# Interleaved sequence tails with whole-tile stores, and one PSUM copy moved forward, in a convolution and channel-mix kernel

## The chip, the cores and the metric

The kernel runs on one core of a Trainium2 chip. The metric is the device time of one execution in microseconds (us). The profiler records a single execution; its span runs from the first to the last instruction of the program. In the tables and views, PE is TensorE (PEld its weight loads), DVE is VectorE, ACT is ScalarE, POOL is GpSimd and SP is SyncE; a letter q behind an engine means its instruction queue, such as a DMA issue.

## The reference: what is computed

The input x has 8 sequences of 4160 tokens with 192 channels in float32. First comes a causal convolution of width 7 whose weights are a softmax, one row for each of 8 heads of 24 channels; then a channel mix.

```python
w = softmax(weight, axis=-1)                     # 8 heads x 7 taps
y[b, s, h, g] = sum_k w[h, k] * x_pad[b, s + k, h, g]    # 6 zeros ahead of each sequence
y_prev = y shifted by one token
xk = mu_k * y + (1 - mu_k) * y_prev
xr = mu_r * y + (1 - mu_r) * y_prev
k = relu(xk @ w_k)                               # 192 -> 1024
v = (k * k) @ w_v                                # 1024 -> 192
out = sigmoid(xr @ w_r) * v                      # float32
```

## The kernel before

The 8 sequences are handled as 4 pairs. The two sequences of a pair lie in the two halves of the partitions: 64 channels each, three channel groups c. Work on a pair goes in steps of 512 tokens, and each step has 8 slots of k product (two banks of PSUM each). Four slots make a *bundle*, and the program is a list of bundles, written out by hand: `bundle_first`, `bundle_second`, and `bundle_rest(b, ns)` for all the others, from b = 2 on. Each engine runs its instructions in the order in which this code issues them. Tables (`early`, `rq`, `xt`, `mix_a`, `mix_b`, `mix_c`, `vq`, `late`) hold for each bundle what else is to be issued at a given place, and `run(table, b)` issues it.

These parts matter here:

- **The convolution.** `load_x` (L112) brings blocks of x into `xb` by DMAs that POOL issues. `conv_half` (L630) calls `conv_mm` (L295, matmuls on L310) for one half of a unit, and after the second half `conv_out` (L342) has ScalarE copy the result to `y` (L356). A small instruction in ScalarE's queue after the first half (L318) lets the second half go on. From there y goes to `yT`, with channels on the partitions: for most groups by a write to DRAM (`y_write`, L379) and a transposing read (`y_read`, L387), both issued by SP; for group 3 by `tr(g, j)` (L392), that is TensorE transposes into PSUM (L401) and copies out of it (L410). The five blocks of group 3 make two calls: j = 0 with four blocks, copied by ScalarE in two pieces, and j = 1 with one block, copied by VectorE.
- **The mix.** `diff` (L435) subtracts neighbouring tokens, `scale` (L466) multiplies by mu one channel group at a time, `add_y` (L472) adds y. All of it is VectorE's. `y_of` (L421) gives the tokens of a step, shifted by k.
- **The k product.** `k_mm` (L492) on TensorE, `k_relu` (L504) on ScalarE into one of four `k_sb` buffers, and `k_square` (L518) on VectorE into `k2`.
- **The r and v products.** `r` (L549, with the sigmoid on L557), `v_rows` in two halves (L577, with an instruction in ScalarE's queue, L585, between them), and `v_out` (L593), where VectorE multiplies v by r; SP then issues two stores, one for each sequence (L601).
- **The PSUM ring.** `ring` has four buffers, tag "k", each of two banks. k, r, v, the convolution and the transposes all take their place from it, and a new tile waits until the engine that reads the old one is done.
- **The tails.** 4160 is 8 times 512 plus 64, so 64 tokens of each sequence are left. `keep_tail(p)` (L417) has POOL copy them, with the token ahead, to `y_tail` at the end of each pair, and the last step (LAST) computes all four pairs at once: 256 columns, which are pair by pair 64 tokens. `shaped` (L428) gives the mix buffers that form. In the end `v_last` (L606) makes four tiles of 128 rows, k = 0 to 3. Tile k holds two pairs of one sequence place, 64 rows each, so each tile is stored by two DMAs of 64 rows (L620): the lower half by SP, the upper half by ScalarE.

In `bundle_rest` the third bundle (b = 2) differs from the rest: it issues the transposes of group 3 after the first half of v, and the convolution halves later. The issue order before the change was: k product, relu and square of slot 0; the `mix_b` table (for b = 2 two scalings of xk); k product, relu and square of slot 1; r; the first half of v; `tr(3, 0)` and `tr(3, 1)`; the k product and relu of slot 2; a convolution half; the second half of v; two more convolution halves; the `mix_c` table (`add_y` among it); the k product of slot 3; the last convolution half.

Of the kernel before, what the change touches and what calls it, by code (L numbers as in the profile page):

```python
# [8 lines left out]
BF16 = mybir.dt.bfloat16  # L9
# [5 lines left out]
def kernel(  # L15
# [11 lines left out]
    nc = tc.nc  # L27

    B, S, D = x.shape
# [3 lines left out]
    P = 128  # L33
    NF = DF // P
    Q = 64
    NC = D // Q
# [6 lines left out]
    TAIL = S % 128  # L43
    NPAIR = B // 2
# [4 lines left out]
    const = ctx.enter_context(tc.tile_pool(name="const", bufs=1))  # L49
# [10 lines left out]
    for p in range(NPAIR):  # L60
# [5 lines left out]
        for L in sizes:  # L66
            ns = L * NF // STEP
# [3 lines left out]
    T0, LAST = S - TAIL, len(steps) - 1  # L71
# [108 lines left out]
    wr = const.tile([P, NC, D], BF16)  # L180
    wv = const.tile([P, NF, D], BF16)

    y_tail = const.tile([P, NC, NPAIR, TAIL + 2], BF16)

    def load_thirds(w, m, n, cs=slice(0, NC)):
        for st in range(2):
# [99 lines left out]
    ys, yTs, y_drams = {}, {}, {}  # L286
# [8 lines left out]
    def conv_mm(g, c, half):  # L295

        nb = groups[g][2]
        if half == 0:
            if c == 0:
                ys[g] = two.tile([P, GB, 2 * D], BF16, tag="y", name="y")  # L300
            conv_ps[g, c] = ring.tile([P, 2, BANK], FP32, tag="k", name="ps_c")
        unit = conv_units(g)[c]
        last = len(unit[0]) - 1
        banks = conv_ps[g, c][:, :, 0 : nb * 2 * G * (last + 1)].rearrange("p i (n s c) -> p i n s c", n=nb, s=2)
        for k in range(last + 1):
            for i in range(2):
                q = slice(i * Q, (i + 1) * Q)
                bank = (i + half) % 2
                h = unit[bank][k]
                nc.tensor.matmul(  # L310
                    out=banks[:, bank, :, :, k * G : (k + 1) * G],
                    lhsT=toe[q, h, :],
                    rhs=xbs[g][q, :nb, :, h * G : (h + 1) * G],
                    start=half == 0 and k == 0,
                    stop=half == 1 and k == last,
                )
        if half == 0:
            nc.scalar.clobber_nop([nc.scalar.lower_ap(conv_ps[g, c])])  # L318
# [73 lines left out]
    def tr(g, j):  # L392

        p, blk0, nb, _, _ = groups[g]
        ps = ring.tile([P, 2, 2 * BANK], BF16, tag="k", name="ps_t")
        todo = range(4 * j, min(nb, 4 * j + 4))
        view = ps[:, :, 0 : 6 * BLK].rearrange("p b (c i t) -> p b c i t", c=3, i=2)
        for i0 in todo[::2]:
            for c in range(3):
                for i in range(i0, min(nb, i0 + 2)):  # L400
                    nc.tensor.transpose(  # L401
                        out=view[:, (i - 4 * j) // 2, c, i % 2, :],
                        in_=ys[g][:BLK, i, c * P : (c + 1) * P],
                        identity=ident[:BLK, :BLK],
                    )

        for i in todo[::2]:
            n = min(2, nb - i)
            c0 = YC + (blk0 + i) * BLK
            (nc.scalar.copy if g == 3 and j == 0 else nc.vector.tensor_copy)(  # L410
                out=yTs[p][:, :, c0 : c0 + n * BLK].rearrange("p c (n t) -> p c n t", n=n),
                in_=view[:, (i - 4 * j) // 2, :, :n, :],
            )
# [2 lines left out]

    def keep_tail(p):  # L417
        c0 = YC + T0 - 1
        nc.gpsimd.tensor_copy(out=y_tail[:, :, p, 0 : TAIL + 1], in_=yTs[p][:, :, c0 : c0 + TAIL + 1])  # L419

    def y_of(s, cs, k):  # L421

        p, t0, L, _, _ = steps[s]
        if s == LAST:
            return y_tail[:, cs, :, k : k + TAIL]
        return yTs[p][:, cs, YC + t0 - 1 + k : YC + t0 - 1 + k + L]

    def shaped(s, t):  # L428
        return t.rearrange("p c (a t) -> p c a t", t=TAIL) if s == LAST else t

    def diff(s, cs=slice(0, 3)):
        L = steps[s][2]
# [43 lines left out]
    def k_mm(n, cs=range(NC)):  # L476


        s, j = slots[n]
        L = steps[s][2]  # L480
        xk = xks[s]
        if cs[0] == 0 and n not in k_ps:
            k_ps[n] = ring.tile([P, 2, BANK], FP32, tag="k", name="ps_k")
        ps = k_ps[n]
        nf = STEP // L

        for c in cs:
            for f in range(nf):
                fs = slice((j * nf + f) * P, (j * nf + f + 1) * P)
                for i in range(2):  # L490
                    r = slice(i * Q, (i + 1) * Q)
                    nc.tensor.matmul(  # L492
                        out=ps[:, i, f * L : (f + 1) * L],
                        lhsT=wk[r, c, fs],
                        rhs=xk[r, c, :L],
                        start=c == 0 and f == 0,
                        stop=c == NC - 1 and f == nf - 1,
                    )

    def k_relu(n):  # L500
        ps = k_ps.pop(n)
        k_sb = four.tile([P, 2 * STEP], BF16, tag="k_sb", name="k_sb")
        k_sbs[n] = k_sb
        nc.scalar.activation(out=k_sb, in_=ps.rearrange("p a b -> p (a b)"), func=AF.Relu)  # L504

    def k_square(n):
        s, j = slots[n]
        L = steps[s][2]
        k_sb = k_sbs.pop(n)
        if j == 0:  # L510
            k2s[s] = three.tile([P, NF, 2 * STEP], BF16, tag="k2", name="k2")
        nf = STEP // L
        i = k_sb
        o = k2s[s][:, j, :]
        if nf > 1:
            i = k_sb.rearrange("p (b f t) -> p f b t", b=2, f=nf)
            o = k2s[s][:, j * nf : (j + 1) * nf, 0 : 2 * L].rearrange("p f (b t) -> p f b t", b=2)
        nc.vector.tensor_tensor(out=o, in0=i, in1=i, op=ALU.mult)  # L518
# [11 lines left out]
    def v_mm(o, s, t):  # L530
        for f in range(NF):
            nc.tensor.matmul(  # L532
                out=o,
                lhsT=k2s[s][:, f, t * P : (t + 1) * P],
                rhs=wv[:, f, :],
                start=(f == 0),
                stop=(f == NF - 1),
            )
# [48 lines left out]
    def tile_of(s, j, k):  # L587
        return k // 2 * (steps[s][2] // P) + 2 * j + k % 2
# [17 lines left out]
    def v_last(s, j):  # L606

        r_sb = r_sbs.pop((s, j))
        o_sb = three.tile([P, 4, D], FP32, tag="o_sb", name="o_sb")
        for k in range(4):  # L610
            ps = ring.tile([P, 2, BANK], FP32, tag="k", name="ps_v")
            v_mm(ps[:, 0, 0:D], s, tile_of(s, j, k))
            nc.vector.tensor_tensor(  # L613
                out=o_sb[:, k, :],
                in0=ps[:, 0, 0:D],
                in1=r_sb[:, k // 2, k % 2 * D : (k % 2 + 1) * D],
                op=ALU.mult,
            )
            for i in range(2):
                (nc.scalar if i else nc.sync).dma_start(  # L620
                    out=out[2 * (2 * (k % 2) + i) + k // 2, T0:S, :], in_=o_sb[i * TAIL : (i + 1) * TAIL, k, :]
                )


    early, rq, xt, mix_a, mix_b, mix_c, vq, late = ({} for _ in range(8))
# [4 lines left out]
    def conv_half(unit, half):  # L630
        if unit is not None:
            conv_mm(*unit, half)
            if half == 1:
                conv_out(*unit, nc.scalar.copy)

    for g, (p, blk0, nb, fb, on_pe) in enumerate(groups):
# [13 lines left out]
        if g > 4:  # L650

            b = {5: 1, 6: 2, 7: 7}.get(g)
            b = first_bundle[first_step[p]] + (-15, -11, -7, -3)[(g - 6) % 4] if b is None else b
# [38 lines left out]
    def run(table, b):  # L692
        for fn, a in table.get(b, ()):
            fn(*a)
# [110 lines left out]
    def bundle_rest(b, ns):  # L805

        units = xt.get(b, []) + [None, None]
        quad = vq.get(b, [None])[0]
        for n in bundles[b - 1][2:]:
            k_square(n)  # L810
        run(mix_a, b)
        k_mm(ns[0])
        k_relu(ns[0])
        k_square(ns[0])
        run(mix_b, b)
        if b > 2:
            conv_half(units[0], 0)
        k_mm(ns[1])
        if b > 2:
            conv_half(units[0], 1)  # L820
        k_relu(ns[1])
        k_square(ns[1])
        run(rq, b)
        if quad:
            v_rows(*quad, 0)
        if b == 2:
            tr(3, 0)
            tr(3, 1)
        k_mm(ns[2])
        k_relu(ns[2])  # L830
        if b == 2:
            conv_half(units[0], 0)
            v_rows(*quad, 1)
            conv_half(units[0], 1)
            conv_half(units[1], 0)
        else:
            conv_half(units[1], 0)
            if quad:
                v_rows(*quad, 1)
                conv_half(units[1], 1)  # L840
        run(mix_c, b)
        k_mm(ns[3])
        if not quad or b == 2:
            conv_half(units[1], 1)
        k_relu(ns[3])
        if quad:
            v_out(*quad)
        run(late, b)
# [53 lines left out]
```

## Time and profile before

| | us |
|---|---|
| median of 7 runs | 420.02 (419.73 to 421.88) |
| the profiled execution's own time | 419.8 |
| its span in the profile | 418.0 |
| TensorE matmuls busy | 407.5 (97%) |
| VectorE busy | 378.2 (90%) |
| ScalarE busy | 347.8 (83%) |
| GpSimd busy | 49.0 (12%) |

The page gives for each group of instructions its line, engine, operation and tile, the busy time, the mean time of one, and the idle time of that engine just ahead of the group with what ended it. The page also follows the chain of work that ended last back from the last instruction, as shares of the span. The timeline lists instructions in order of time: start, length, engine, line, operation, and in brackets the idle time of the engine ahead of it. Instructions of one engine overlap a little, so a start says more than a start and a length. A DMA has two times: that of its issue in a queue, and that from issue to landing. The rows for the stores at the end and for the y tails are these: the eight stores of L620 are 48 KB each, four from each queue, and land after 1.9 to 2.5 us; the three VectorE operations on `y_tail` take 0.55 to 0.57 us each; the four copies of `keep_tail` take 0.36 to 0.49 us on POOL.

### The profile page before, as it was taken

To read this page: it belongs to the slowest core of one execution; us is meant where nothing else is said; L and a number is where in the kernel's file an instruction comes from. 1 tells how busy PE (TensorE), PEld (TensorE's weight loads), DVE (VectorE), ACT (ScalarE), POOL (GpSimd) and SP (SyncE) were. 2 spreads that over 40 slices of the span, in tenths; PEclk is the share of its full clock that TensorE was granted. 3 is DMA by queue.
4 is the path that set the end of the run, shared out by engine and by line. 5 is a ranking of instruction groups with operands and counts; after the bars stand their busy time and mean duration, and the time that the engine had idled before them with its cause. 6 is when DMAs were issued, how large, how long until landed. Compare 5 with 4: busy or idle time off the path is not lost.

```text
span 418.0 us, 16366 instructions
## 1 busy us (share of the span) xinstructions
PE 407.5 (97%) x7136; PEld 316.1 (76%) x7136; DVE 378.2 (90%) x674; ACT 347.8 (83%) x408; POOL 49.0 (12%) x73
## 2 busy tenths in 40 slices
PE   7989999999999999999999999999999999999995
PEld 3667777777887778778777877777777788777795
DVE  5888799999999999999999999999999999999983
ACT  5989898898898889888888888898898788887771
POOL 6650002102030100202012010201000000000000
PEclk9999999999999999999999999999999999999998
DMA  9998779958599694959769693898945554421124
GB/s 148 193 190 159 186 187 189 232 140 164 132 191 230 155 193 123 146 162 186 180 149 193 182 175 128 146 220 147 179 111 154 144 138 124 118 78 57 60 79 115
DMA packets 134746, 64.59 MB, mean 155 GB/s; under 512 B 84990, under 2 KB 134674, under 8 KB 134674
## 3 DMA queue, kind: packets, MB, share of 16 engines
q1 hardware_dynamic: 95908, 48.28, 44.9%
q0 software_dynamic: 37872, 14.66, 30.8%
q8 instruction: 56, 0.92, 0.9%
q10 hardware_dynamic: 894, 0.61, 0.5%
q14 instruction: 16, 0.13, 0.1%
HBM read 29.89 MB, written 36.99 MB: 160 GB/s over the span
## 4 chain that ended last, share of the span: by engine, by line
PE 90%; ACT 2%; issue 1%; DVE 0%; ACTq 0%
PE ps_v L577 39%; PE ps_k L492 37%; PE ps_r L549 7%; PE ps_c L310 5%; ACT k_sb L504 1%; PE ps_v L532 1%; ACT y L356 0%; DVE o_sb L593 0%; DVE o_sb L613 0%; ACTq L356 0%; ACTq L318 0%; ACTq L585 0%
## 5 line engine op out<-in xcount | busy, mean ns | idle before, releaser
L504 ACT ACTIVATE k_sb<-ps_k 128x1024 bf16<-128x1024 f32 x260 | 260.9, 1039 | 53.2 <-PE ps_k L492 53.1
L492 PE MATMUL ps_k<-xk,wk 64*128 64x512 bf16 (+1 forms) x1632 | 200.2, 367 | 0.7 <-DVE xk L472 0.3
L518 DVE TENSOR_TENSOR k<-k_sb 128x1024 bf16<-128x1024 bf16 x260 | 177.7, 688 | 14.9 <-ACT k_sb L504 7.9
L577 PE MATMUL ps_v<-wv,k 64*128 64x192 bf16 x4032 | 188.8, 243 | 0.6 <-ACT k_sb L504 0.4
L577 PEld LDWEIGHTS <-k 64*128 64x128 bf16 x4032 | 172.4, 94 | 13.7 <-issue 1.4
L492 PEld LDWEIGHTS <-wk 64*128 64x128 bf16 x1632 | 88.0, 94 | 51.1 <-issue 1.2
L593 DVE TENSOR_TENSOR o_sb<-ps_v,r_sb 128x768 f32<-128x768 f32 x64 | 61.3, 957 | 12.4 <-PE ps_v L577 4.9
L557 ACT ACTIVATE r_sb<-ps_r 128x768 bf16<-128x768 f32 x65 | 54.6, 842 | 0.0
L356 ACT CAST y<-ps_c 120x960 bf16<-120x960 f32 (+4 forms) x67 | 50.7, 787 | 3.2 <-PE ps_c L310 3.2
L126 POOL DMA_DIRECT2D xb<-in_x_dram x34 | 30.6, 902 | 194.2 <-PE ps_c L310 93.0
L549 PEld LDWEIGHTS <-xr 64*128 64x128 bf16 x780 | 36.1, 94 | 11.2 <-issue 0.4
L549 PE MATMUL ps_r<-wr,xr 64*128 64x192 bf16 x780 | 44.0, 243 | 0.0
L310 PE MATMUL ps_c<-xb,toe 64*128 64x480 bf16 (+2 forms) x240 | 39.2, 335 | 1.1 <-DVE yT L410 0.8
L466 DVE TENSOR_SCALAR xr<-d,mu 128x512 bf16<-128x512 bf16 (+1 forms) x102 | 35.6, 352 | 0.0
L466 DVE TENSOR_SCALAR xk<-d,mu 128x512 bf16<-128x512 bf16 (+1 forms) x99 | 32.8, 358 | 0.1
L435 DVE TENSOR_TENSOR d<-yT 128x1536 bf16<-128x1536 bf16 (+3 forms) x37 | 31.4, 848 | 0.9 <-ACT yT L340 0.9
L472 DVE TENSOR_TENSOR xr<-xr,yT 128x1536 bf16<-128x1536 bf16 (+1 forms) x33 | 31.0, 940 | 1.1
L472 DVE TENSOR_TENSOR xk<-xk,yT 128x1536 bf16<-128x1536 bf16 (+2 forms) x34 | 30.5, 897 | 0.1
L310 PEld LDWEIGHTS <-toe 64*128 64x128 bf16 x240 | 13.5, 94 | 13.0 <-issue 2.1
L419 POOL COPY y_tail<-yT 128x195 bf16<-128x195 bf16 x4 | 1.8, 456 | 68.5 <-DMA yT<-y_dram 68.5
L108 POOL MEMSET xb<- 32x384 bf16 x3 | 1.2, 408 | 45.0 <-PE ps_k L492 43.7
L330 PEld LDWEIGHTS <-xb 128*32 128x32 bf16 (+3 forms) x264 | 4.3, 102 | 2.7 <-issue 1.7
(52 smaller groups left out, 62.2 us busy)
## 6 DMA issues: line engine op xcount, KB each, us to landing
out_dram<-o_sb SPq DMA_DIRECT2D x128, 192.0 KB, 2.7
y_dram<-y SPq DMA_DIRECT2D x10, 900.0 KB, 6.4
xb<-in_x_dram POOLq DMA_DIRECT2D x14, 480.0 KB, 7.9
xb<-in_x_dram POOLq DMA_DIRECT2D x6, 432.0 KB, 8.2
xb<-in_x_dram POOLq DMA_DIRECT2D x10, 192.0 KB, 5.9
y_dram<-y SPq DMA_DIRECT2D x3, 450.0 KB, 6.1
y_dram<-y SPq DMA_DIRECT2D x1, 810.0 KB, 5.8
wk<-in_moe_w_k_dram POOLq DMA_DIRECT2D x4, 192.0 KB, 6.5
```

The source lines that it names most:

```text
L310: nc.tensor.matmul(out=banks[:, bank, :, :, k * G : (k + 1) * G], lhsT=toe[q, h, :], rhs=xbs[g][q, :nb, :, h * G : (h + 1) * G], start=hal ...
L356: copy(out=bass.AP(tensor=y.tensor, offset=y.offset + d0, ap=[y.ap[0], [d1 - d0, 2], [2 * D, nb], [Q, 2], [1, n]],), in_=bass.AP(tensor=ps ...
L435: nc.vector.tensor_tensor(out=shaped(s, diffs[s][:, cs, :L]), in0=y_of(s, cs, 1), in1=y_of(s, cs, 0), op=ALU.subtract)
L466: nc.vector.tensor_scalar(out=t[:, c, :L], in0=diffs[s][:, c, :L], scalar1=mu[:, i, c : c + 1], scalar2=None, op0=ALU.mult)
L472: nc.vector.tensor_tensor(out=o, in0=o, in1=y_of(s, sl, 0), op=ALU.add)
L492: nc.tensor.matmul(out=ps[:, i, f * L : (f + 1) * L], lhsT=wk[r, c, fs], rhs=xk[r, c, :L], start=c == 0 and f == 0, stop=c == NC - 1 and f ...
L504: nc.scalar.activation(out=k_sb, in_=ps.rearrange("p a b -> p (a b)"), func=AF.Relu)
L518: nc.vector.tensor_tensor(out=o, in0=i, in1=i, op=ALU.mult)
L549: nc.tensor.matmul(out=ps[:, i, k * D : (k + 1) * D], lhsT=xr[q, c, ts], rhs=wr[q, c, :], start=c == 0, stop=c == NC - 1,)
L557: nc.scalar.activation(out=r_sbs[s, j], in_=ps[:, :, 0 : 2 * D], func=AF.Sigmoid)
L577: nc.tensor.matmul(out=v_ps[s, j][:, bank, k * D : (k + 1) * D], lhsT=k2s[s][q, f, t * P : (t + 1) * P], rhs=wv[q, f, :], start=half == 0 ...
L593: nc.vector.tensor_tensor(out=o_sb.rearrange("p (b t) d -> p b (t d)", b=2), in0=v_ps.pop((s, j)), in1=r_sbs.pop((s, j)), op=ALU.mult,)
```

## The change

There are two independent parts.

First, in the third bundle, the square of slot 1 and the `mix_b` table are issued after the two calls of `tr` instead of ahead of r. On VectorE the order from the square of slot 0 on was: two scalings of xk, the square of slot 1, the copy of `tr(3, 1)`, `add_y`. It becomes: the copy, the square of slot 1, the two scalings, `add_y`. The order on the other engines is the same.

Second, the layout of the tails. `y_tail` had the axes channel group, pair, token; it gets channel group, pair of pairs, token, and which of the two. So a column of the last step is (pair of pairs, token, which), and a tile of 128 rows in `v_last` holds the tokens of two pairs in turn. One DMA stores a whole tile, with a DRAM side that steps token by token and inside that between the two sequences. Tiles 0 and 2 are stored by SP, tiles 1 and 3 by ScalarE.

```diff
-    y_tail = const.tile([P, NC, NPAIR, TAIL + 2], BF16)
+    y_tail = const.tile([P, NC, NPAIR // 2, TAIL + 1, 2], BF16)
...
-        nc.gpsimd.tensor_copy(out=y_tail[:, :, p, 0 : TAIL + 1], in_=yTs[p][:, :, c0 : c0 + TAIL + 1])
+        nc.gpsimd.tensor_copy(out=y_tail[:, :, p // 2, :, p % 2], in_=yTs[p][:, :, c0 : c0 + TAIL + 1])
...
-            return y_tail[:, cs, :, k : k + TAIL]
+            return y_tail[:, cs, :, k : k + TAIL, :].rearrange("p c a t b -> p c a (t b)")
...
-        return t.rearrange("p c (a t) -> p c a t", t=TAIL) if s == LAST else t
+        return t.rearrange("p c (a t) -> p c a t", t=2 * TAIL) if s == LAST else t
...
-            for i in range(2):
-                (nc.scalar if i else nc.sync).dma_start(
-                    out=out[2 * (2 * (k % 2) + i) + k // 2, T0:S, :], in_=o_sb[i * TAIL : (i + 1) * TAIL, k, :]
-                )
+            (nc.scalar if k % 2 else nc.sync).dma_start(
+                out=bass.AP(
+                    tensor=out.tensor,
+                    offset=out.offset + ((4 * (k % 2) + k // 2) * S + T0) * D,
+                    ap=[[D, TAIL], [2 * S * D, 2], [1, D]],
+                ),
+                in_=o_sb[:, k, :],
+            )
...
-        run(mix_b, b)
         if b > 2:
+            run(mix_b, b)
             conv_half(units[0], 0)
         k_mm(ns[1])
         if b > 2:
             conv_half(units[0], 1)
         k_relu(ns[1])
-        k_square(ns[1])
+        if b > 2:
+            k_square(ns[1])
         run(rq, b)
         if quad:
             v_rows(*quad, 0)
         if b == 2:
             tr(3, 0)
             tr(3, 1)
+            k_square(ns[1])
+            run(mix_b, b)
         k_mm(ns[2])
```

## The prediction

> **What bounds the kernel now.** I read the page first, then the chain of waits, then the idle time by engine, and then two stretches of the timeline: the third bundle and the end. The page's totals and chain:
>
> ```profile
> span 418.0 us, 16366 instructions
> ...
> PE 407.5 (97%) x7136; PEld 316.1 (76%) x7136; DVE 378.2 (90%) x674; ACT 347.8 (83%) x408; POOL 49.0 (12%) x73
> ...
> PE 90%; ACT 2%; issue 1%; DVE 0%; ACTq 0%
> ```
>
> The reader is to see that TensorE sets the time: 90% of the chain is its work. The chain cut to 60 to 410 us holds TensorE lines alone, and over 28 to 410 us TensorE's idle time, asked by releaser, sums to 0.8 us (0.4, 0.2 and 0.2). So there are two places where time can be had: a stretch in which TensorE stands still, and the stretch after its last matmul, which starts at 413.15 us and ends near 413.4, while the span runs to 418.0. The change touches one of each. The largest single idle stretch of TensorE after 20 us is in the third bundle (TensorE's timeline; start, length, engine, line, in brackets the idle time ahead and what ended it):
>
> ```profile
> 24.72 0.96 PE L401 MATMUL ps_t<-ident,y 120*128 120x120 bf16 x15
> 25.84 0.82 PE L492 MATMUL ps_k<-xk,wk 64*128 64x512 bf16 x6 [0.16 <-ACT r_sb L557]
> 27.50 0.38 PE L310 MATMUL ps_c<-xb,toe 64*128 64x480 bf16 x2 [0.83 <-DVE yT L410]
> 27.70 1.50 PE L577 MATMUL ps_v<-wv,k 64*128 64x192 bf16 x32
> ```
>
> The convolution at 27.50 needs a place in the PSUM ring of four, and takes the one that VectorE's copy of the last transposes (L410) gives back. VectorE's own row of work shows why that copy is late:
>
> ```profile
> 25.27 0.68 DVE L518 TENSOR_TENSOR k<-k_sb 128x1024 bf16<-128x1024 bf16 x1
> 25.87 0.72 DVE L466 TENSOR_SCALAR xk<-d,mu 128x512 bf16<-128x512 bf16 x2
> 26.51 0.68 DVE L518 TENSOR_TENSOR k<-k_sb 128x1024 bf16<-128x1024 bf16 x1
> 27.11 0.33 DVE L410 COPY yT<-ps_t 128x360 bf16<-128x360 bf16 x1
> 27.37 0.95 DVE L472 TENSOR_TENSOR xk<-xk,yT 128x1536 bf16<-128x1536 bf16 x1
> 29.29 0.96 DVE L593 TENSOR_TENSOR o_sb<-ps_v,r_sb 128x768 f32<-128x768 f32 x1 [0.98 <-issue]
> ```
>
> The transposes ended at 24.72 + 0.96 = 25.68; the copy stood behind two scalings and a square until 27.11. VectorE then waits 0.98 us for the v product that the late convolution held up. The end (ScalarE's and SyncE's queues):
>
> ```profile
> 412.05 2.53 ACTq L620 DMA_DIRECT2D out_dram<-o_sb  x4
> ```
> ```profile
> 411.78 0.92 SPq L601 DMA_DIRECT2D out_dram<-o_sb  x2
> 412.79 2.72 SPq L620 DMA_DIRECT2D out_dram<-o_sb  x4
> ```
>
> The last multiplication ends at 413.43 + 0.36 = 413.79. ScalarE issues its last store at 414.02, but SyncE, kept by the v_out pair (L601) until 412.70, then issues four stores of 0.56 to 0.66 us in a row and begins its last one at 414.96. That lands 1.94 us later, at 416.90, and 1.12 us of closing work follow.
>
> **Part 1, the third bundle.** Nothing is added: the order of six VectorE instructions changes, and TensorE, ScalarE and the queues keep theirs. The copy now follows the square at 25.27, so it can start at 25.87, when that one lets go (the transposes ended 0.19 us before). It ends at 25.87 + 0.33 = 26.20, and with the 0.06 us that lay between copy and matmul before (27.11 + 0.33 = 27.44 to 27.50) the place is free at 26.26. TensorE's six k matmuls issue in three steps of about 0.215, until 25.84 + 0.65 = 26.49. So the convolution starts at 26.49 instead of 27.50: **-1.0 us**.
>
> What is late next? (a) The square and the two scalings move 0.26 us later (copy to next start: 27.37 - 27.11). Behind them add_y still starts at 27.37 and ends at 28.32; its reader, the k product of the next bundle, moves from 30.30 to 29.3, so 1 us is left. The square's ScalarE buffer comes round four relus later. (b) VectorE is free at 28.24; the v product's end moves from 29.2 to 28.2, so L593 moves from 29.29 to about 28.3. VectorE's 0.98 us of idle time is just used up: this also caps the gain. (c) ScalarE is busy until 28.03 and then idle for 1.40 us ahead of the y copy at 29.44; that copy can go 1.0 us earlier and leaves 0.4. (d) The x block that this convolution reads: POOL issued its last load at 15.1 and it took 11.0 us, so it landed at about 26.1. The weight load carrying that wait ran at 26.27, 0.10 us behind its neighbour, so it lost nothing; but only some 0.15 us are to spare, where 1.2 us were. If that landing is late by d, the gain is 1.0 - (d - 0.15). Bounds: 1.0 where it isn't late, nothing where it is late by 1.15; the row says it wasn't, so I take 1.0. The other inputs have room: the next x block's loads landed by 30.5, are read at 38.3 and would be read at 37.3.
>
> Is it kept to the end? Between 28 and 60 us TensorE, ScalarE and VectorE wait for one another in turn; each link starts from work that is itself 1.0 us earlier. The one fixed delay inside is the trip of y through DRAM (written at 39.07, read back at 45.12, landed 7.3 us later at 52.4, for a VectorE operation at 53.18); it starts 1.0 us earlier too. From 60 us on the chain is TensorE's alone, and an earlier start is an earlier end.
>
> **Part 2, the tails.** keep_tail on POOL writes every second element: four copies of 0.36 to 0.49 us on an engine that is 12% busy, the last at 361.9 against a reader at 394.8; even ten times that costs nothing. VectorE's three operations on y_tail took 0.57, 0.55 and 0.56 us. The Trainium skill, VectorE: DVE Perf Modes, section "Mode 2×_1P — pack two bf16 into one 32-bit read", asks for step 1 and 4-byte alignment; the old layout reads one operand an odd number of elements off, the new one does not, and by the rule these three would each lose 0.4 us in the old form. The rows differ: 768 elements of yT, with the same odd offset, took 0.55, and 1536 took 0.96, so the slope is 0.41 us for 768, and the odd offset has no slower rate to lose. I take 0. Bounds: one slope, 0.4 us each way for each; all three lie ahead of idle stretches of VectorE (0.76 at 401.15, 1.04 at 406.89) or of an operand needed much later, so also 0 on the path.
>
> The stores: eight become four, k = 0 and 2 on SyncE, 1 and 3 on ScalarE. SyncE: k = 0 at 412.79 as before, k = 2 by 413.6, done by 414.3. ScalarE: the last multiplication ends at 413.79 and 0.23 us later, as before, the last store is issued: 414.02. It is now the last of all. Its landing is not in the trace at this size (96 KB). Nearest rows: the 48 KB stores of this end took 1.94 to 2.47, the 192 KB store at 411.78 took 2.03. I take 2.1, so it lands at 416.1 instead of 416.9: **-0.8 us**; from the ends, -0.4 (2.47) to -0.9 (1.94). For the size alone, the Trainium skill, DMA: Bandwidth & Descriptors, section "Anatomy of one DMA — SWDGE (gpsimd) path", gives 2.0 us and the bytes at 436 GB/s, fitted to another queue; by it a doubled store would land an estimated 0.1 us later and the gain be 0.1 smaller; the 192 KB row shows no such growth.
>
> **Sum.** 1.0 + 0.8 = 1.8 us off the profiled execution's own time of 419.8 (span 418.0 and 1.8 around it): 418.0. The median of the seven runs, 420.02, is 0.2 above that execution, so a median of 418.0 to 418.2; I say 418.1, which is 0.45% less. A measurement of this kernel can tell about 0.3%, 1.26 us, from no change.
>
> **Rivals.**
> 1. *Only one gain counts.* The x block lands late in most executions, or VectorE's copy has to wait for the transposes, and the stall comes back under another name: 419.8 - 0.8 - (0 to 0.4) = 418.6 to 419.2. For: 0.15 us to spare on a load that took 11.0. Against: the weight load did not wait. Or the end falls away and only 1.0 is left: 419.0. Chance 0.30, nearly all within 0.3%.
> 2. *Nothing arrives*: ScalarE or VectorE between 28 and 60 us takes the microsecond back, since VectorE's slack is used up to 0.0, and the new store lands no sooner: 419.4 to 420.0. Against: their idle stretches there (0.2 to 1.2 us) are waits for earlier work that moves too. Chance 0.05.
> 3. *Slower*: the new store, whose DRAM side jumps between two sequences at each row, is not spread over the DMA engines. Its 128 rows of 768 B, at the 0.04 us that such a packet took at the end by the trace's packet records, are 5.1 us on one engine against 0.3 on sixteen: landing 4.8 us later, and 418.0 + 4.8 = 422.8. On n engines it is 5.1/n; the 1.8 us are gone, and it decides, with two engines or fewer. Against: the 48 KB stores of 64 rows kept to 1.94 us, and a first dimension of 64 rows in DRAM and 128 in SBUF is no shorter than theirs. Chance 0.04.
>
> The forecast has 0.61. **Range** 417.6 (both gains at their bounds, 1.0 + 0.9, and 0.3 less for the profiled run's spread) to 419.3 (rival 1 with its ends). Faster by over 0.3%: 0.63; within: 0.33; slower: 0.04.
>
> **What would show it.** Part 1: no idle time ahead of L310 near 26.5, VectorE's copy at 25.9, L593 near 28.3 without a gap, and the last matmul near 412.1 instead of 413.15. If the weight load of L310 waits instead, it is the x block. Part 2: last issue on ScalarE's queue 0.23 us behind the last multiplication, and from that multiplication's end to the span's end 3.4 us instead of 4.2. The prediction is wrong if the last matmul has not moved, or if the store takes over 2.5 us.

## The result, and the profile after

| | before | after |
|---|---|---|
| median, us | 420.05 (419.58 to 422.02, 47 runs) | 418.37 (417.78 to 420.03, 20 runs) |
| span of the profiled execution, us | 418.0 | 416.6 |

The ratio of the two is 0.9959, with a 95% interval of 0.9951 to 0.9967: 0.41% faster, where 418.1 us and 0.45% were forecast. From the page of the changed kernel, the totals and the chain:

```profile
span 416.6 us, 16358 instructions
...
PE 407.4 (98%) x7136; PEld 316.6 (76%) x7136; DVE 379.1 (91%) x674; ACT 347.7 (83%) x408; POOL 49.0 (12%) x73
...
PE 91%; ACT 3%; DVE 3%; issue 1%; POOL 0%; ACTq 0%; POOLq 0%
```

The work is the same to 0.1 us on TensorE; 1.4 us of the span are gone, and they are idle time of TensorE. The third bundle, TensorE's timeline of the changed kernel:

```profile
25.04 0.96 PE L401 MATMUL ps_t<-ident,y 120*128 120x120 bf16 x15
26.16 0.82 PE L492 MATMUL ps_k<-xk,wk 64*128 64x512 bf16 x6 [0.16 <-ACT r_sb L557]
26.81 0.38 PE L310 MATMUL ps_c<-xb,toe 64*128 64x480 bf16 x2
27.01 1.50 PE L577 MATMUL ps_v<-wv,k 64*128 64x192 bf16 x32
```

The bracket behind L310 is gone. From the first transpose to the convolution it was 27.50 - 24.72 = 2.78 us and is 26.81 - 25.04 = 1.76 (with unrounded starts): 1.02 us less. But the transposes themselves stand 0.32 us later than in the profile before, which is why the span shows 1.4 and not 1.8 us; the first experiment asks whose doing that is. VectorE beside it:

```profile
25.59 0.68 DVE L518 TENSOR_TENSOR k<-k_sb 128x1024 bf16<-128x1024 bf16 x1
26.19 0.33 DVE L410 COPY yT<-ps_t 128x360 bf16<-128x360 bf16 x1
26.44 0.68 DVE L518 TENSOR_TENSOR k<-k_sb 128x1024 bf16<-128x1024 bf16 x1
27.04 0.61 DVE L466 TENSOR_SCALAR xk<-d,mu 128x512 bf16<-128x512 bf16 x2
27.68 0.96 DVE L472 TENSOR_TENSOR xk<-xk,yT 128x1536 bf16<-128x1536 bf16 x1
28.60 0.96 DVE L593 TENSOR_TENSOR o_sb<-ps_v,r_sb 128x768 f32<-128x768 f32 x1
```

The copy follows the first square at once, and L593 (v times r) follows `add_y` without its 0.98 us of waiting. The end, ScalarE's queue and then SyncE's:

```profile
411.82 1.87 ACTq L619 DMA_DIRECT2D out_dram<-o_sb  x2
```
```profile
411.09 0.95 SPq L601 DMA_DIRECT2D out_dram<-o_sb  x2
412.14 1.32 SPq L619 DMA_DIRECT2D out_dram<-o_sb  x2
```

Now ScalarE's last store, begun at 413.14, is the last of all, and SyncE is done before it.

To compare executions, four differences are read from each trace: the *bundle stretch*, from the first transpose of the third bundle to the convolution behind it; the *middle*, from there to the start of the last matmul; the *end stretch*, from there to the end of the span; and within that the *closing*, from the last store's landing on. The last matmul's start is near its end, since the closing matmuls follow each other at 0.08 us.

| kernel | first transpose at | bundle stretch | middle | end stretch | last store issued after the last matmul's start | closing |
|---|---|---|---|---|---|---|
| before | 24.72 | 2.78 | 385.65 | 4.87 | 1.81 | 1.12 |
| after | 25.04 | 1.76 | 385.66 | 4.12 | 0.67 | 1.38 |
| after, again | 24.72 | 1.76 | 385.65 | 4.25 | 0.67 | 1.37 |
| after, third time | 24.73 | 2.06 | 385.76 | 4.08 | 0.67 | 1.38 |
| part 1 only | 24.70 | 1.76 | 385.70 | 4.89 | 1.80 | 1.14 |
| part 2 only | 24.49 | 2.74 | 385.69 | 4.06 | 0.67 | 1.37 |
| last store on the last semaphore | 27.02 | 1.77 | 385.70 | 3.67 | 0.67 | 0.95 |
| the same, again | 25.26 | 1.76 | 385.76 | 3.80 | 0.67 | 0.94 |
| copy between | 25.10 | 2.13 | 385.69 | 4.12 | 0.67 | 1.37 |
| old halves, SyncE relieved | 26.88 | 1.76 | 385.71 | 4.64 | 1.52 | 1.19 |

The middle column is the strongest evidence that what the bundle gains is kept: 385.65 to 385.76 us in ten profiles, whatever stands ahead of it.

### The profile page after: what moved, and what is told of

Same layout as the page of the kernel before. It is cut to its first block, busy times and chain, and to the rows that moved or that the text cites. A ratio compares the mean times of both kernels' runs of the same rounds, so it can differ in the third digit from the quotient of the medians.

```text
span 416.6 us, 16358 instructions
## 1 busy us (share of the span) xinstructions
PE 407.4 (98%) x7136; PEld 316.6 (76%) x7136; DVE 379.1 (91%) x674; ACT 347.7 (83%) x408; POOL 49.0 (12%) x73
## 4 chain that ended last, share of the span: by engine, by line
PE 91%; ACT 3%; DVE 3%; issue 1%; POOL 0%; ACTq 0%; POOLq 0%
PE ps_v L577 40%; PE ps_k L492 38%; PE ps_r L549 7%; PE ps_c L310 5%; ACT k_sb L504 2%; PE ps_v L532 1%; DVE k L518 1%; ACT y L356 1%; PE warm L702 1%; DVE d L435 0%; POOL xb L126 0%; ACT yT L340 0%; DVE xk L448 0%; DVE xk L466 0%; DVE xk L472 0%
## 5 line engine op out<-in xcount | busy, mean ns | idle before, releaser
L593 DVE TENSOR_TENSOR o_sb<-ps_v,r_sb 128x768 f32<-128x768 f32 x64 | 61.2, 957 | 11.2 <-PE ps_v L577 4.5
L310 PE MATMUL ps_c<-xb,toe 64*128 64x480 bf16 (+2 forms) x240 | 39.2, 334 | 0.3
L310 PEld LDWEIGHTS <-toe 64*128 64x128 bf16 x240 | 13.5, 94 | 11.8 <-issue 0.9
L330 PEld LDWEIGHTS <-xb 128*32 128x32 bf16 (+3 forms) x264 | 4.8, 109 | 2.5 <-issue 1.5
```

The source lines that it names most:

```text
L310: nc.tensor.matmul(out=banks[:, bank, :, :, k * G : (k + 1) * G], lhsT=toe[q, h, :], rhs=xbs[g][q, :nb, :, h * G : (h + 1) * G], start=hal ...
L593: nc.vector.tensor_tensor(out=o_sb.rearrange("p (b t) d -> p b (t d)", b=2), in0=v_ps.pop((s, j)), in1=r_sbs.pop((s, j)), op=ALU.mult,)
```

## The experiments

### The changed kernel again (after_again)

> The changed kernel once more, beside its parts and on their chip. Its first profile has the 15 transposes of the third bundle at 25.04 us where the kernel before has them at 24.72, although nothing ahead of them differs. Theory A: those 0.32 us are a matter of the single execution (when the first x blocks land); then this profile lies anywhere between 24.7 and 25.1 and the span between 416.3 and 416.7, with 4.1 us from the start of the last matmul to the end. Theory B: the change itself costs them; then 25.04 again, to 0.05. Ratio to before 0.996.

Measured: the transposes at 24.72, span 416.4, ratio 0.9950 (0.9937 to 0.9962). Theory A holds: the 0.32 us belong to one execution. Against the kernel before this profile has 1.6 us less span: 1.01 in the third bundle (the last matmul starts at 412.14 instead of 413.15) and 0.62 in the end stretch.

### Each part alone (part1_only, part2_only)

The two parts of the diff, each taken alone onto the kernel before.

> Only the copy ahead of the square and the two scalings; tails and stores as before. Theory A (the stall at 27.50 was the copy's lateness and its 1.0 us is kept to the end): no idle time ahead of the convolution, 1.77 us from the start of the third bundle's first transpose to the convolution's start (2.78 before), end stretch unchanged at 4.87 us from the last matmul's start; ratio 0.9976, about -1.0 us. Rival (the engines take it back between 28 and 60 us): the stall goes but the ratio stays between 0.999 and 1.0.

> Only the tails; the third bundle as before. Theory A (parts add up): the end stretch is 4.14 us instead of 4.87, so -0.7 us, ratio 0.9983, and the stall of 0.83 us ahead of the convolution is there. Rival (what the first part gives is all there is, the store's gain is lost in its closing): ratio 0.9995 to 1.0.

Part 1 alone: ratio 0.9983 (0.9970 to 0.9997), median 418.95 against 420.14. Its stretches are as expected, 1.76 and 4.89. The ratio is less of a gain than the 0.9976 that was expected, and its interval, which holds that, also reaches into the rival's range (0.999 to 1.0). So the time alone does not settle it; the profile does: the middle is 385.70 us, where the kernel before has 385.65, and nothing was taken back there. TensorE's timeline of part 1 alone, and of part 2 alone:

```profile
24.70 0.96 PE L401 MATMUL ps_t<-ident,y 120*128 120x120 bf16 x15
25.82 0.82 PE L492 MATMUL ps_k<-xk,wk 64*128 64x512 bf16 x6 [0.16 <-ACT r_sb L557]
26.47 0.38 PE L310 MATMUL ps_c<-xb,toe 64*128 64x480 bf16 x2
```
```profile
24.49 0.96 PE L401 MATMUL ps_t<-ident,y 120*128 120x120 bf16 x15
25.61 0.82 PE L492 MATMUL ps_k<-xk,wk 64*128 64x512 bf16 x6 [0.16 <-ACT r_sb L557]
27.23 0.38 PE L310 MATMUL ps_c<-xb,toe 64*128 64x480 bf16 x2 [0.80 <-DVE yT L410]
```

Part 2 alone: ratio 0.9974 (0.9964 to 0.9985), median 419.03; the stall is back and the end stretch is 4.06. The parts add up as far as times known to some 0.1% can show it: 0.17% and 0.26% are 0.43%, against 0.41% measured together. Neither rival is left: the first part's gain is not taken back, by the profile, and the second part's is not lost, by time and profile.

### The copy half way back (copy_between)

```diff
         k_relu(ns[1])
-        if b > 2:
-            k_square(ns[1])
+        k_square(ns[1])
...
             tr(3, 1)
-            k_square(ns[1])
             run(mix_b, b)
```

> The changed kernel, but with the copy behind the square of slot 1 and ahead of the two scalings: half way back. Theory A (the copy's end releases the convolution, one for one past TensorE's own time): the copy starts 0.60 us later, which uses up the 0.23 us between its release and the convolution and then costs 0.37: 2.1 us from the first transpose to the convolution's start (1.76 with the change, 2.78 before), ratio 0.997. Rival (any order with the copy ahead of the scalings does): 1.76 and 0.996.

Measured: bundle stretch 2.13, ratio 0.9973 (0.9958 to 0.9989). TensorE's timeline of this kernel:

```profile
25.10 0.96 PE L401 MATMUL ps_t<-ident,y 120*128 120x120 bf16 x15
26.22 0.82 PE L492 MATMUL ps_k<-xk,wk 64*128 64x512 bf16 x6 [0.16 <-ACT r_sb L557]
27.23 0.38 PE L310 MATMUL ps_c<-xb,toe 64*128 64x480 bf16 x2 [0.19 <-DVE yT L410]
```

Three places of the copy give three stalls: 0.83 behind the scalings and the square, 0.19 behind the square alone, none ahead of both. The bracket counts from the end of the last k matmul, which the profile models; that is 0.17 us later than the next matmul could start, so the loss in starts is 2.13 - 1.76 = 0.37, as worked out beforehand. The ratio's interval holds both 0.997 and the rival's 0.996; it is the stretch that decides.

### The next wait: the x block (xb_late, xb_late_old_order)

The prediction named the x block of the freed convolution as what is late next. A first attempt, wv_twice, issued the load of wv twice in the prologue:

> The changed kernel with the load of wv issued twice in the prologue, ahead of the x block that the freed convolution reads; the second brings the same data again. In the profiles so far that block lands at 25.6 to 26.1 us and wv takes 2.0 us of the queue. Theory A (the block's landing is the next wait, as the rival in the prediction has it): it lands near 27.9, the convolution starts at about 28.1, 3.4 us behind the first transpose, and the ratio goes back to about 0.9995; the weight load of that convolution waits. Theory B (nothing depends on it): 1.76 us and 0.996.

It was a poor experiment: POOL's second load into the same tile had to wait for the first to land (POOL stood still for 6.9 us), and the v product ahead of the transposes then waited itself. From 27.2 us on, behind that wait, TensorE's granted clock was 0.50 for 3.4 us, and the same v product took 2.74 us instead of 1.50. The ratio was 1.0081 (1.0063 to 1.0099), out of what either theory said. TensorE's waits of this kernel, longest first (the columns are the wait in us in total, how many, and the longest):

```profile
PE ps_v L577 <- DMA wv<-in_moe_w_v_dram: 4.1, 1, 4.1
PE ps_c L310 <- DMA xb<-in_x_dram: 0.5, 1, 0.5
```

The second line is the wait that was looked for, but not its price. So the load was repeated into a tile that nobody reads, with the new order and with the old one:

```diff
         load_wv()
+        nc.gpsimd.dma_start(out=spare, in_=moe_w_v.rearrange("(f p) d -> p f d", p=P))
         x_tile(4)
```

> The changed kernel with one more load of w_v, into a tile that nobody reads, just ahead of the x block of the freed convolution: 2.0 us of the queue, so the block should land near 27.7 to 28.3 instead of 25.6 to 26.7, and no product waits for the extra load itself. Theory A (the block's landing is the next wait, one for one): the convolution's weight load waits for it, the convolution starts 0.15 us behind the landing, near 28.1, some 3.3 us behind the first transpose (1.76 with the change), and the ratio goes to about 1.0. Theory B (the block has slack): 1.76 us and 0.996.

> The same extra load in the kernel before. Theory A: the old order waits until 27.5 anyway, so of a landing at 28.1 it loses only some 0.6 us: ratio 1.0015, 3.3 us from the first transpose to the convolution as in the other run (2.78 before). Theory B: 2.78 us and 1.0.

The two timelines, the new order first (the added lines move L310 to L311 and the others alike):

```profile
24.76 0.96 PE L402 MATMUL ps_t<-ident,y 120*128 120x120 bf16 x15
25.88 0.82 PE L493 MATMUL ps_k<-xk,wk 64*128 64x512 bf16 x6 [0.16 <-ACT r_sb L558]
28.23 0.38 PE L311 MATMUL ps_c<-xb,toe 64*128 64x480 bf16 x2 [1.53 <-DMA xb<-in_x_dram]
```
```profile
24.62 0.96 PE L402 MATMUL ps_t<-ident,y 120*128 120x120 bf16 x15
25.74 0.82 PE L493 MATMUL ps_k<-xk,wk 64*128 64x512 bf16 x6 [0.16 <-ACT r_sb L558]
28.49 0.38 PE L311 MATMUL ps_c<-xb,toe 64*128 64x480 bf16 x2 [1.93 <-DMA xb<-in_x_dram]
```

The block landed at 28.10 and at 28.36, and each convolution began 0.13 us behind. Theory A holds: one for one, and with the block this late both orders wait for the same thing and part 1 is worth nothing. The stretches are 3.47 and 3.87 us, where 3.3 was expected for both; they differ by as much as the landings do against the transposes. The ratios agree with it: 1.0004 (0.9990 to 1.0017) with the change and 1.0021 (1.0005 to 1.0038) without, 0.17% apart, which is what the end stretch alone (some 0.75 us) would leave, though the intervals overlap.

This also happens by itself. In the other profiles of the same prologue, those with the table's first transposes below 26 us, the block landed between 25.6 and 26.7. The third profile of the changed kernel had the latest, and there it cost 0.30 us; TensorE's weight loads in that execution:

```profile
25.62 0.56 PEld L492 LDWEIGHTS <-wk 64*128 64x128 bf16 x6
26.76 0.13 PEld L310 LDWEIGHTS <-toe 64*128 64x128 bf16 x2 [0.58 <-issue]
```

The weight load of L310, which had run 0.10 us behind the end of its neighbours in the kernel before, stood until 26.76, 0.1 us behind the landing at 26.66; so the bundle stretch is 2.06 and not 1.76.

### SyncE's queue or the stores' size (halves_relieved)

Part 1 with the old layout and its eight half-tile stores, of which ScalarE takes five:

```diff
-                (nc.scalar if i else nc.sync).dma_start(
+                (nc.scalar if i or k == 0 else nc.sync).dma_start(
```

> Part 1 with the old layout and the old eight half-tile stores, but ScalarE issues both stores of tile 0, so that SyncE, kept by the pair ahead, has three left and not four. Theory A (the end was late by SyncE's queue of issues, not by the stores' size): ScalarE issues five at about 0.65 us each, the last begins 1.45 us behind the last matmul's start instead of 1.80; 4.55 us to the end where part 1 alone has 4.89, so 0.3 us less than that, ratio 0.9975. Rival (it is the number or size of the stores that lands late): 4.9 us still, last landing over 2.3 us.

Measured: ratio 0.9967 (0.9954 to 0.9979), last store 1.52 us behind the last matmul's start, end stretch 4.64 against 4.89 of part 1 alone. The last store landed after 1.9 us, as before. So the old end was late by the issues in line on a queue: one store less in the longer line was worth 0.25 us in the profile, with no change of a store's size or of their number. The ratio alone would not tell it, since its interval overlaps with that of part 1 alone (0.9970 to 0.9997). ScalarE's queue of this kernel and of part 1 alone:

```profile
413.25 3.17 ACTq L620 DMA_DIRECT2D out_dram<-o_sb  x5
```
```profile
411.07 2.53 ACTq L620 DMA_DIRECT2D out_dram<-o_sb  x4
```

Five stores in 3.17 us and four in 2.53: 0.63 each. This shows a step of the prediction to be wrong: with four, ScalarE's last store does not begin 0.23 us behind the last multiplication because a signal takes that long, but because the one ahead of it has just been issued (before the change that one held the queue from 413.36 to 413.93, and the last began at 414.02). With two stores in ScalarE's queue it begins 0.03 us behind (413.11 to 413.14).

### The order of the closing waits (lane_last, lane_again)

A semaphore tells SyncE that a store has landed; the stores take eight semaphores in turn, and at the close SyncE waits for all eight. The run is the changed kernel, with seven 4 KB stores to scratch tensors added late in the kernel, in the sixty-first bundle:

```diff
+        if b == 60:
+            for i in range(7):
+                nc.sync.dma_start(out=pads[i][:, :], in_=ident[:, 0:16])
```

> The changed kernel with seven stores of 4 KB to a scratch tensor late in the kernel, which move the last store from semaphore 0 of the eight that the stores take in turn to semaphore 7. At the close SyncE waits for the eight one after the other, some 0.06 us each; in the changed kernel the last landing (415.20) is that of the first of them, and 1.40 us follow to the end, 1.12 before the change. Theory A (the order of these waits is what the end lost): some 1.0 us from the last landing to the end, so 0.4 us less than the changed kernel, ratio 0.995. Rival (the closing is as long wherever the last store stands): 1.4 us, ratio 0.996, or worse by what the seven stores cost.

Measured: closing 0.95, end stretch 3.67; in the second run 0.94 and 3.80. In the page's terms, SyncE's instructions behind the last landing, in the changed kernel and in this one (second run):

```profile
L904 SPq EVENT_SEMAPHORE  x10: 17/28/28, 415.2 to 416.5; - x10
```
```profile
L909 SPq EVENT_SEMAPHORE  x3: 17/17/28, 415.7 to 416.5; - x3
```

Ten against three, and 7 at 0.06 us are 0.43. Before the change it was six (closing 1.12), and with ScalarE's five stores it was seven (closing 1.19); both lie on the same line. So theory A holds in the profile. In the time it is not settled. The first run had a ratio of 0.9949 (0.9933 to 0.9966) and a median of 417.99 against 418.10 of the changed kernel on the same chip; it was repeated beside the changed kernel:

> The kernel with the last store on the last of the eight semaphores once more, beside the changed kernel on one chip. If the order of the closing waits is worth its 0.4 us in the unprofiled time too: median 0.4 us under the changed kernel's, ratio 0.995 against 0.996. If the spread of the prologue (24.5 to 27.0 us at the first transpose in the profiles so far) hides it, the medians differ by under 0.2 us, and only the end stretch tells (3.7 us against 4.1 to 4.25).

> The changed kernel, for comparison with the kernel beside it: ratio 0.9955, end stretch 4.1 to 4.25 us.

Medians 418.21 against 418.45, ratios 0.9955 (0.9943 to 0.9968) and 0.9962 (0.9948 to 0.9975). Both comparisons point the same way, by 0.11 and 0.24 us where the profiles say 0.43, and the intervals overlap: that this kernel is the faster of the two is likely and not shown.

## Why the prediction was right, point by point

**The bundle, -1.0 us: right in place, mechanism and size.** The stretch fell by 1.01 to 1.02 us in the undisturbed profiles, the copy began when the first square let go, and L593's gap closed. The item-by-item search for what is late next held: `add_y`, ScalarE and VectorE were in time, and the x block, with its 0.15 us to spare, was the next wait; it took 0.30 us back in one profile of the changed kernel out of three. That rival was real, as a part of the spread and not as the rule.

**Kept to the end: right.** The middle is the same in all profiles to 0.1 us.

**The end, -0.8 us: right in sum, by luck: two errors nearly cancel.** From the last matmul's start, the last issue was forecast at 0.87 us (414.02 - 413.15) and came at 0.67, since ScalarE's own line of issues had been taken for a signal's delay. The landing was forecast at 2.1 and took 2.0 to 2.2. The closing was taken to stay at 1.12 us and took 1.37 to 1.38: the last store now stands first in SyncE's list of waits. In sum -0.62 to -0.81 against the kernel before. The rule that was weighed for the landing, the Trainium skill's DMA: Bandwidth & Descriptors, section "Anatomy of one DMA — SWDGE (gpsimd) path", had an estimated 0.1 us for the doubled size. The last 48 KB stores took 1.93 to 1.95 and the last 96 KB ones 2.0 to 2.2, so the doubled size came with 0.1 to 0.3 us. By that estimate a last store would take 2.04 us (1.94 + 0.1), by the 192 KB row 2.03: both lie at the low end, so the runs do not choose between them.

**The tails' layout, 0: right, with one reading wrong.** VectorE's three operations took 0.55, 0.55 and 0.56 us (0.57, 0.55 and 0.56 before). The prediction has all three read an operand an odd number of elements off in the old layout. By the code only `diff` did (its operand with k = 1); the two `add_y` read k = 0, at even places in both layouts. So the alignment that the skill's VectorE: DVE Perf Modes asks for is tried by one operation, and it went from 0.57 to 0.55 us, not by 0.4; POOL's copies with their step of two took 0.41 to 0.43.

**The slower rival did not come**: the stores to two sequences in turn land like the others.

**418.1 against 418.37.** The measured terms add to 1.5 to 1.8 us in the three profiles of the changed kernel, where 1.8 was forecast, and the first medians differ by 1.68. What is left is within what one median differs from the next (418.37, 418.10 and 418.45 for the same kernel).

## What to carry to other kernels

Where one engine bounds the kernel, look for the few stretches in which it stands still, and for who gives back the buffer it waits for; an instruction that frees a shared buffer belongs ahead of work with slack on its engine, and the price can be read off beforehand, down to where the next wait caps it. At the end of a kernel, count the issues in line on each queue behind the last result, not the bytes: here one 96 KB store on a free queue beat two of 48 KB behind others. And before a gain of that kind is booked, look for the input that had slack only because of the stall that is to go.

## What the runs showed of the hardware that was not expected

- At the close SyncE waits for the stores' eight completion semaphores one after another, about 0.06 us each, in a fixed order; the closing was 0.94 us with the last store on the last of them and 1.38 with it on the first.
- At the end of the kernel an issue of a store took the queue 0.53 to 0.68 us for 48 KB from 64 partitions and 0.55 to 0.65 for 96 KB from 128; of the last two of 192 KB, the first took 0.37 and the second 0.47 to 0.80. So the issue did not grow with the bytes.
- The first x load can hold up the prologue. In five of thirteen profiles it held up ScalarE's first conversion, by 0.12 to 1.70 us; the two longest, 1.45 and 1.70, are the table's 27.02 and 26.88, and their spans are 418.2 and 419.0. The wait is not all of it: their transposes are 2.2 to 2.3 us later than those of the kernel before, and TensorE took 4.58 us for 166 matmuls of L330 where it took 3.82 for 168 there. Nor does it explain the 25.04 and 25.10 of two profiles in which nothing held that conversion up. ScalarE's rows with the longest of these waits, in the kernel with five stores on ScalarE:

```profile
5.99 0.20 ACT L222 ACTIVATE w_sig<-w_exp 1x1 f32<-1x1 f32 x1
7.89 1.25 ACT L225 CAST xb<-x_f 128x576 bf16<-128x576 f32 x2 [1.70 <-DMA x_f<-in_x_dram]
```

A delay of 2.2 us is the size of the spread in the unprofiled times of most kernels here (418.68 to 421.03 for part 1 alone), and larger than the whole change. That it makes this spread isn't shown, and why that load is sometimes late was not tried.
